# All the engines' orders of a fused attention and gated-MLP kernel written anew

## The chip, the core and the metric

The kernel runs on one core of a Trainium2 chip. The core has a matrix engine (TensorE, "PE" in the profile, with its weight loads as "PEld"), a vector engine (VectorE, "DVE"), a scalar engine (ScalarE, "ACT"), a general engine (GpSimd, "POOL") and a sync engine (SyncE, "SP") that here issues nearly all DMA transfers. Each engine works through its own list of instructions in order and waits on semaphores for the others. SBUF is the working memory, PSUM the eight banks in which TensorE leaves its results. The metric is the device time of one execution in microseconds (us).

## The reference

A linear attention with decay feeds a gated MLP with a spatial mixing matrix. With B = 4 batches, H = 8 heads, S = 768 positions, D = 64 per head, model width 512 and d_ff 1024:

```python
# attention, in blocks of 64 positions
intra = einsum('bhij,bhjd->bhid', einsum('bhic,bhjc->bhij', qb, kb) * Dmask, vb)
inter = einsum('bhid,bhde->bhie', qb * lam_pow, kv_state)
out[:, :, sl] = intra + inter
kv_state = lam_block * kv_state + einsum('bhsd,bhse->bhde', kb * rev_pow, vb)
# gated MLP on x = attention with its heads side by side (4 x 768 x 512)
h = maximum(x @ w_in, 0);  u, v = h[..., :512], h[..., 512:]
v_n = (v - mean(v)) / sqrt(var(v) + 1e-6)
v_s = einsum('ts,bsd->btd', w_spatial, v_n) + b_spatial[None, :, None]
result = (u * v_s) @ w_out
```

All inputs and the result are float32; TensorE multiplies in bfloat16.

## The kernel before, in words

The work is cut into twelve **steps** of 256 positions, three to a batch: step n belongs to batch n // 3. A step loads its keys, queries and values (512 KB each), scales keys and queries by the decay, transposes both, forms scores, masks them, multiplies by the values, adds the carried state, and sends the result through W_in. Each input has three buffers and most intermediates two, used in turn, so that a load waits until the input of three steps before has been read.

Nothing plans at run time. The order stands in the text `ORDER` (lines 16 to 85): each word is one operation, its numbers, and the engine that does it (T = TensorE, D = VectorE, A = ScalarE, P = GpSimd, S = SyncE). The program reads the words from front to back, so an engine's list is the words with its letter, in the order of the text:

```python
        for token in ORDER.split():
            name, *args, e = token.split(".")
            ops[name](e, *map(int, args))
```

The words that matter here (first number the step n, or for the MLP's second half the batch; the last numbers of a T word are PSUM banks):

- **LK, LQ, LV** n (line 196): load keys, queries, values. **WH.0, WH.1** (L253): the two pieces of W_in's v half; **WH.2, WH.3**: the two pieces of its u half. **WQ.0 to 5** (L274): six pieces of W_spatial, 384 KB each; **WP** (L283): W_out. All on SP's queue. The pieces land in float32 in shared buffers and are cast by **CW** (v half), **CX** (u half), **WC** (W_spatial), **WX** (W_out), lines 181 to 185 by the engine. WQ.0 and WQ.1 reuse the buffer of WH.0 and WH.1, WQ.4 and WQ.5 that of WH.2 and WH.3, so that their issue waits for the casts.
- **lam, BR** (ACT's queue): decay rates and the spatial bias. LB, LN, LL, LX make the decay tables; BB, BE spread the bias; **FL** (L309) are matmuls on ones whose result is not used.
- **KM, QM** (L331): keys or queries times decay, on D or P. **TK, TQ** (L366): their transposes on TensorE, **EK, EQ** their copies out of PSUM; from step 7 on **DK, DQ** (L344, L348) transpose by DMA instead, issued by SP. **VC, VD**: cast of the values.
- **SC** (L396) scores, **MK** (L401) mask, **AV** (L459, L468) values, **KP** (L425) state products, **SX, SY, SA** copies and sums of the state. **EX** copies the step's result out as x transposed; **FN** is a copy of one element that orders the two banks.
- **PV, EV** (L493, L498/L500): x times the v half, and its relu. **BN, RA, RD, RB** (L508/509, L513, L518, L523): mean, variance, square root, reciprocal, product of both. **VN** (L532 on D, L529 on A): the normalised v. **PU, EU** (L544, L498/L500): the same for u. **GN** (L536) makes POOL wait for a VN.
- **WT, EW** (L556): transposes of W_spatial and their copies; the last number before the bank is the half of the positions. **GP** copies the bias into a bank, **PW** (L570) adds W_spatial times v to it, **GM** (L576) multiplies by u. A batch has eight PW groups, and each needs all six VN of its batch. **PO, EO** (L581), in halves **PH, EH** (L590): W_out and the copy out; **ST, SH** (L604, L600): the stores.

Of the kernel before, what the change touches and what calls it, by code (L numbers as in the profile page):

```python
# [643 lines left out]
```

## Time and profile before

| what | value |
|---|---|
| median of three runs | 143.64 us (143.48 to 143.75) |
| the profiled execution, device time | 144.71 us |
| its span on the engines | 143.0 us |
| TensorE busy, share of the span | 133.8 us, 94% |
| VectorE, ScalarE, GpSimd busy | 115.3, 82.8, 51.9 us |
| moved by DMA | 33.60 MB |

In the rows of the trace the first two columns are start and duration in us; then come engine, line, operation, what is written and read, the shape, and a count where neighbours are merged. A bracket tells how long the engine had stood idle and what released it. Ends of matmuls are modelled and overlap their successors, so the duration of one matmul is longer than its share of the engine. In a row by stage the columns are the stage, its length, the busy time of PE, PEld, DVE, ACT and POOL with counts, the granted clock of TensorE as a share of full speed, the busy share of the DMA engines and the GB/s that they moved. A list by line gives minimum, median and maximum duration in ns, the first and last start, and the shape.

### The profile page before, as it was taken

What the parts mean: (1) busy time and instruction counts of PE and PEld (TensorE: products, weight loads), DVE (VectorE), ACT (ScalarE), POOL (GpSimd) and SP (SyncE); (2) the same over time, 40 slices, a digit from 0 to 9 for tenths busy, and PEclk for the clock granted to TensorE, in tenths of its full rate; (3) what the DMA queues carried; (4) which work ended last, traced back from release to release, by engine and by line L of the source; (5) the groups of instructions that cost most, each with busy time, mean ns of one, the idle gap of its engine ahead of it and who ended that gap; (6) DMA issues with size and microseconds to landing.
All of it is one profiled execution on the core that took longest, in us unless ns stands there. A gap on an engine that the chain in (4) does not pass through costs nothing.

```text
span 143.0 us, 4741 instructions
## 1 busy us (share of the span) xinstructions
PE 133.8 (94%) x1999; PEld 87.7 (61%) x2014; DVE 115.3 (81%) x236; ACT 82.8 (58%) x158; POOL 51.9 (36%) x61
## 2 busy tenths in 40 slices
...
GB/s 87 347 347 346 386 323 315 294 339 313 337 302 344 259 288 324 285 166 290 293 0 78 49 282 354 180 142 238 276 257 126 177 5 117 406 139 0 78 324 185
DMA packets 54617, 33.60 MB, mean 235 GB/s; under 512 B 11715, under 2 KB 49859, under 8 KB 54596
## 3 DMA queue, kind: packets, MB, share of 16 engines
...
q8 instruction: 15, 0.25, 0.7%
...
HBM read 24.38 MB, written 6.29 MB: 215 GB/s over the span
## 4 chain that ended last, share of the span: by engine, by line
PE 83%; DVE 9%; ACT 3%; issue 2%; DVEq 0%; ACTq 0%
PE ps L570 21%; PE ps L581 14%; PE ps L493 13%; PE ps L544 11%; PE ps L396 5%; PE ps L366 5%; PE ps L309 4%; PE ps L468 4%; PE ps L425 3%; PE ps L459 2%; DVE st L508 2%; DVE qc L331 2%; DVE kc L331 2%; DVE vn L532 1%; DVE win_sb L183 1%
## 5 line engine op out<-in xcount | busy, mean ns | idle before, releaser
L570 PE MATMUL ps<-wt_sb,vn 128*128 128x384 bf16 x192 | 33.7, 326 | 0.5 <-ACT vn L529 0.3
L331 POOL TENSOR_TENSOR kc<-k_in,lv 128x512 bf16<-128x512 f32 x20 | 20.5, 1043 | 30.0 <-PE ps L493 11.5
L401 DVE TENSOR_TENSOR a_sb<-ps,m 128x1024 bf16<-128x1024 f32 x24 | 28.4, 1211 | 0.7 <-PE ps L425 0.6
L570 PEld LDWEIGHTS <-vn 128*128 128x128 bf16 x192 | 18.3, 98 | 12.3 <-ACT vn L529 0.6
L544 PE MATMUL ps<-xT,win_sb 128*128 128x256 bf16 x192 | 23.6, 273 | 0.5 <-DVE win_sb L183 0.5
L331 POOL TENSOR_TENSOR qc<-q_in,lqn 128x512 bf16<-128x512 f32 x18 | 19.3, 1090 | 10.2 <-DMA q_in<-in_q_dram 5.2
L493 PE MATMUL ps<-win_sb,xT 128*128 128x512 bf16 x89 | 22.3, 379 | 0.4
L581 PE MATMUL ps<-wout_sb,gT 128*128 128x512 bf16 x84 | 22.1, 379 | 0.4
L576 DVE TENSOR_TENSOR gT<-ps,uT 128x384 bf16<-128x384 f32 x32 | 16.8, 551 | 7.1 <-PE ps L570 6.7
L544 PEld LDWEIGHTS <-win_sb 128*128 128x128 bf16 x192 | 18.4, 98 | 5.1 <-DVE win_sb L183 0.7
L181 ACT ACTIVATE ps<-bsp 128x384 f32<-128x384 f32 x23 | 11.2, 490 | 10.7 <-DVE gT L576 6.7
L508 DVE BATCH_NORM_STATS2 st<-vh 128x6 f32<-128x512 bf16 x24 | 16.2, 676 | 1.1 <-ACT vh L498 1.1
L181 ACT ACTIVATE o_sb<-ps 128x512 f32<-128x512 f32 (+1 forms) x14 | 8.0, 579 | 15.4 <-PE ps L581 14.6
L493 PEld LDWEIGHTS <-xT 128*128 128x128 bf16 x96 | 8.8, 98 | 9.6 <-ACT xT L181 0.8
L498 ACT ACTIVATE vh<-ps 128x512 bf16<-128x512 f32 x20 | 11.7, 600 | 4.9 <-PE ps L493 3.2
L181 ACT ACTIVATE xT<-ps 128x512 bf16<-128x512 f32 x20 | 11.0, 598 | 5.8 <-PE ps L468 5.7
L581 PEld LDWEIGHTS <-gT 128*128 128x128 bf16 x92 | 8.7, 98 | 8.6
L498 ACT ACTIVATE uT<-ps 128x512 bf16<-128x512 f32 x20 | 11.7, 590 | 2.0 <-PE ps L544 2.0
L468 PE MATMUL ps<-a_sb,vb 64*64 64x128 bf16 x384 | 10.2, 220 | 0.3 <-issue 0.3
L396 PE MATMUL ps<-qT,kT 64*64 64x128 bf16 x384 | 9.7, 226 | 0.0
L309 PE MATMUL ps<-ones 128*128 128x256 bf16 x32 | 7.5, 368 | 1.6 <-DVE ones L305 1.5
L185 POOL CAST vb<-v_in 128x1024 bf16<-128x1024 f32 (+1 forms) x6 | 5.8, 965 | 7.8 <-PE ps L468 7.8
...
## 6 DMA issues: line engine op xcount, KB each, us to landing
...
```

The costliest lines, as they stand in the source:

```text
L181: nc.scalar.activation(out=o, in_=i, func=AF.Copy)
L331: vec(e).tensor_tensor(out=dst[n % NCA][:, u].rearrange("p u m o d -> p o (u m) d"), in0=src[n % NIN].rearrange("p (o u) m d -> p o u m d" ...
L396: nc.tensor.matmul(out=pa[o][row(c), w, j], lhsT=kT[n % NTR][row(o), u, j, c * Q64:(c + 1) * Q64], rhs=qv(n, o, u, c), start=(w == 0 and j ...
L401: nc.vector.tensor_tensor(out=a_sb[n % NA][:, i].rearrange("p o w j x -> p o w (j x)"), in0=ps[:, b0:b1 + 1:b1 - b0].rearrange("p o (w y) ...
L468: nc.tensor.matmul(out=po[c ^ o][row(w), c, i], lhsT=vb[n % NCA][row(c), 4 * o + u, j, :], rhs=a[row(c), i, o, w, j, :], start=(r == 0 and ...
L493: nc.tensor.matmul(out=bank(b), lhsT=x[:, slot(c, g)], rhs=win_sb[:, g, DH:DFF], start=(g == 0), stop=(g == NCH - 1))
L498: nc.scalar.activation(out=o, in_=i, func=AF.Relu)
L508: nc.vector.bn_stats(out=st6[p2][:, t], in_=vh[p2][:, t])
L544: nc.tensor.matmul(out=pu[:, f2].rearrange("p (c x) -> p c x", c=2), lhsT=win_sb[:, g, f * P:(f + 1) * P], rhs=x[:, slot(0, g):slot(1, g) ...
L570: nc.tensor.matmul(out=bank(b)[:, 0:HW], lhsT=vn[bb % 2][:, s, f * P:(f + 1) * P], rhs=wt_sb[:, s, i * HW:(i + 1) * HW], start=False, stop ...
L576: nc.vector.tensor_tensor(out=gT[bb % 2][:, f, cols], in0=bank(b)[:, 0:HW], in1=uT[bb % 2][:, f, cols], op=ALU.mult)
L581: nc.tensor.matmul(out=bank(b), lhsT=gT[bb % 2][:, f, t * P:(t + 1) * P], rhs=wout_sb[:, f, :], start=(f == 0), stop=(f == NCH - 1))
```

## The change

Only the text `ORDER` changes. It has 719 words before and after, 213 of them on TensorE with the same matmuls, 81 on SP with the same transfers, and 54 on POOL. Some operations change their engine: DVE gets 215 instead of 211, ACT 156 instead of 160 (among them: CX.0 from POOL to DVE and CX.1 from DVE to POOL; CW.1 from ACT to POOL, CW.3 from ACT to DVE; KM and QM of step 1 from POOL to DVE, QM.3 from DVE to POOL, KM.3.0 from POOL to DVE; VC.2 and VC.3 from DVE to POOL, VC.4, VC.7 and VC.11 from POOL to ACT; EV.0.1, EU.0.1, EW.2.0 and VN.0.0 from ACT to DVE; WC.4 from ACT to DVE, WC.3 from DVE to ACT). The banks are dealt out anew too.

On SP's queue: queries of step 0 go ahead of its keys, and the first values come sixth instead of fifth. WH.2 and WH.3 stand directly behind the values of step 2, WQ.1, WQ.2, WQ.0 behind them, then the queries of step 3, then WQ.3, WQ.4, WQ.5, and only then keys and values of step 3. Before, the order there was LV.2, LQ.3, WH.3, WQ.0, WQ.1, WQ.2, WH.2, LK.3, LK.4, WQ.3, WQ.4, WQ.5. Further down, the values and queries of step 9 move from in front of DQ.7 to behind DQ.8, the values of step 11 from in front of DK.11 to behind DQ.11. On ACT's queue lam goes ahead of the bias. The 32 filler matmuls are spread otherwise, none behind TK.2.0.

```diff
 ORDER = """
-LK.0.S LQ.0.S LQ.1.S LK.1.S LV.0.S LQ.2.S BR.A lam.A tab.0.A msk.P idn.P posk.P one.D row.D FL.2.256.0.1.T
-FL.2.256.5.1.T FL.2.256.3.1.T FL.2.256.4.1.T FL.2.256.1.1.T FL.1.256.3.1.T FL.2.256.5.1.T LB.1.T LN.1.A eps.D mkc.D
-LL.D LX.A KM.0.0.D QM.0.0.D QM.0.1.D KM.0.1.D FL.1.256.6.1.T BB.1.2.T BB.0.0.T TQ.0.0.3.T FL.2.256.1.1.T TK.0.0.6.T
-tab.1.A BE.1.2.A VC.0.A TQ.0.1.4.T TK.0.1.5.T EQ.0.0.3.D EK.0.0.6.D EQ.0.1.4.D EK.0.1.5.D BE.0.0.D FL.1.256.1.1.T
...
-LV.1.S WH.0.S WH.1.S LV.2.S LQ.3.S WH.3.S VD.1.1.P CW.2.P EQ.1.0.1.D SX.0.D EQ.1.1.5.A SY.0.2.A EK.1.1.3.A
...
-MK.1.0.1.2.D MK.1.1.5.6.D EQ.2.0.0.A VD.1.0.A EK.2.1.4.A KP.1.2.T AV.1.0.0.1.T SY.1.2.D SA.1.0.D FN.1.0.1.D
-EK.2.0.3.A SC.2.1.4.5.T FL.1.256.6.1.T CW.0.A CW.1.A SC.2.0.2.3.T AV.1.1.0.1.T WQ.0.S WQ.1.S WQ.2.S WH.2.S WC.0.P
-WC.1.P WC.2.P MK.2.1.4.5.D MK.2.0.2.3.D SA.1.1.D VC.2.D CW.3.A EX.1.1.1.A EX.1.0.0.A PV.0.1.6.T PV.0.0.4.T
-PV.1.0.5.T KP.2.6.T AV.2.0.2.3.T SA.2.0.D EV.0.1.6.A FN.2.2.3.A EV.0.0.4.A GP.0.0.0.1.A PV.1.1.6.T FL.1.256.0.1.T
-AV.2.1.2.3.T EX.2.0.2.A QM.3.1.D QM.3.0.D TQ.3.2.4.T CX.1.D PU.0.1.0.T PU.1.1.2.T EX.2.1.3.A EV.1.1.6.A BN.0.0.D
-EV.1.0.5.A BN.0.1.D RA.0.A EU.0.1.0.A EU.1.1.2.A PV.2.0.3.T PV.2.1.6.T BN.1.1.D BN.1.0.D EV.2.0.3.A RA.1.A
-EV.2.1.6.A WT.0.0.3.T WT.2.0.5.T EW.2.0.5.A PU.2.1.2.T WT.1.0.0.T BN.2.0.D RD.1.D BN.2.1.D VN.1.1.D RD.0.D RB.0.D
-EW.0.0.3.A RA.2.A VN.0.0.A CX.0.P PU.2.0.6.T EU.2.0.6.A VN.0.1.A EW.1.0.0.D RD.2.D LK.3.S PU.1.0.5.T PU.0.0.3.T
-VN.2.0.D VN.1.0.D VN.2.1.D LK.4.S WQ.3.S EU.1.0.5.D GP.0.2.0.6.D EU.2.1.2.A GP.0.1.0.5.A EU.0.0.3.A GP.0.3.0.2.A
-KM.3.0.P WQ.4.S WQ.5.S LV.3.S LQ.4.S LQ.5.S LV.4.S KM.4.0.P QM.4.0.P QM.4.1.P QM.5.0.P QM.5.1.P VC.4.P PW.0.0.0.1.T
-KM.4.1.D KM.3.1.D WC.3.D GM.0.0.0.1.D PW.0.1.0.5.T PW.0.2.0.6.T TK.3.2.0.T WC.4.A EQ.3.2.4.A EK.3.2.0.A WC.5.D
-GM.0.1.0.5.D GM.0.2.0.6.D WT.2.1.3.T WT.0.1.1.T EW.0.1.1.D WP.S VC.3.D EW.2.1.3.A GP.0.1.1.6.A PW.0.3.0.2.T
-WT.1.1.4.T LK.5.S GM.0.3.0.2.D SC.3.1.0.1.T KP.3.5.T SC.3.0.2.3.T MK.3.1.0.1.D EW.1.1.4.A PW.0.1.1.6.T TK.4.2.0.T
...
-MK.5.0.1.2.D KM.6.0.P KM.6.1.P LK.7.S LQ.7.S LQ.6.S KM.7.1.P QM.7.0.P QM.6.0.P QM.6.1.P EX.4.1.0.A EX.4.0.6.A
-PV.4.1.0.T PV.4.0.4.T AV.5.0.1.5.T BN.3.1.D FN.5.1.5.D KP.6.2.T AV.5.1.1.5.T EV.4.0.4.A PO.0.2.4.T PO.0.0.6.T
-EV.4.1.0.A EX.5.1.5.A EX.5.0.1.A BN.3.0.D PV.5.1.0.T PU.5.1.5.T PV.5.0.1.T KM.7.0.P LV.7.S LV.9.S LQ.8.S LQ.9.S
-LK.8.S LV.8.S EO.0.2.4.D EU.3.0.3.A BN.4.1.D RA.3.A RD.3.D GP.1.2.0.4.D GP.1.1.0.3.A SY.6.2.A EV.5.1.0.D
...
-BN.6.1.D PV.6.0.5.T PO.1.2.2.T VC.9.A KM.9.1.P KM.9.0.P PV.7.1.6.T EV.7.1.6.D PV.7.0.4.T AV.8.0.0.1.T KP.9.3.T
-EV.6.0.5.A GP.2.3.1.6.A EV.7.0.4.A FN.8.0.1.D AV.8.1.0.1.T BN.6.0.D BN.7.0.D EX.8.1.1.A EX.8.0.0.A PU.6.0.5.T
...
-RB.8.D LQ.10.S LK.10.S ST.0.0.S LV.10.S DK.9.S LQ.11.S VN.7.0.D VN.6.1.D VN.8.0.D VN.8.1.D GP.2.3.0.5.A EU.8.0.4.A
...
+lam.A BR.A tab.0.A LQ.0.S LK.0.S LK.1.S LQ.1.S LQ.2.S LV.0.S idn.P posk.P msk.P one.D eps.D row.D FL.1.256.5.1.T
+FL.2.256.1.1.T LB.3.T FL.2.256.6.1.T FL.2.256.2.1.T FL.1.256.0.1.T FL.2.256.4.1.T FL.2.256.6.1.T FL.1.256.6.1.T
+FL.1.256.2.1.T LN.3.A BB.0.4.T BB.1.3.T LL.D LX.A QM.0.1.D KM.0.0.D QM.0.0.P BE.0.4.D mkc.D KM.0.1.P TQ.0.1.1.T
+TK.0.1.4.T KM.1.0.D TQ.0.0.6.T TK.0.0.5.T TK.1.0.0.T BE.1.3.A EQ.0.1.1.A EK.0.1.4.A QM.2.1.P QM.2.0.P KM.1.1.D
...
+FL.1.256.4.1.T MK.1.1.0.1.D KP.1.4.T EK.2.0.5.D EQ.2.1.2.D SA.1.0.D WH.1.S CW.2.P LV.2.S AV.1.0.0.1.T EQ.2.0.6.A
+EK.2.1.3.A CW.0.A FN.1.0.1.D SC.2.0.5.6.T SC.2.1.2.3.T WH.2.S WH.3.S WQ.1.S WQ.2.S WQ.0.S AV.1.1.0.1.T EX.1.1.1.A
+EX.1.0.0.A SY.1.4.D SA.1.1.D CW.3.D PV.0.0.4.T PV.1.1.1.T PV.0.1.0.T MK.2.0.5.6.D MK.2.1.2.3.D EV.0.0.4.A VC.2.P
+CX.1.P WC.1.P WC.2.P WC.0.P AV.2.0.5.4.T KP.2.6.T PV.1.0.6.T BN.0.0.D SA.2.0.D CX.0.D tab.1.A FN.2.5.4.A
+AV.2.1.5.4.T EV.1.0.6.A EV.0.1.0.D BN.1.0.D BN.0.1.D EX.2.1.4.A EX.2.0.5.A EV.1.1.1.A BN.1.1.D PU.1.0.2.T PU.0.0.3.T
+EU.0.0.3.A PU.0.1.5.T PV.2.1.6.T RA.1.A RA.0.A EU.0.1.5.D GP.0.0.0.1.A EV.2.1.6.A RD.1.D RD.0.D EU.1.0.2.D VN.1.1.D
+RB.0.D PV.2.0.0.T PU.2.0.4.T WT.1.0.3.T WT.0.0.5.T PU.1.1.6.T EV.2.0.0.A VN.0.1.A GP.0.2.0.2.A BN.2.1.D EW.1.0.3.D
+BN.2.0.D LQ.3.S QM.3.0.P QM.3.1.P WT.2.0.0.T PU.2.1.3.T EU.2.0.4.A EW.0.0.5.A RA.2.A WQ.3.S WC.3.A GP.0.1.0.4.A
+TQ.3.2.5.T WQ.4.S WQ.5.S EU.1.1.6.A EQ.3.2.5.A GP.0.1.1.6.A EU.2.1.3.A VN.0.0.D EW.2.0.0.D RD.2.D VN.1.0.D VN.2.0.D
+VN.2.1.D LK.3.S PW.0.0.0.1.T WC.5.D WC.4.D GM.0.0.0.1.D LV.3.S LQ.4.S VC.3.P QM.4.0.P LK.4.S KM.4.0.P KM.4.1.P
+GN.2.1.P KM.3.0.D GP.0.3.0.3.A PW.0.2.0.2.T WT.0.1.0.T PW.0.1.0.4.T WT.1.1.5.T WT.2.1.1.T EW.0.1.0.D GM.0.2.0.2.D
+KM.3.1.D GM.0.1.0.4.D PW.0.3.0.3.T TK.3.2.0.T QM.4.1.D GM.0.3.0.3.D EW.1.1.5.A EW.2.1.1.A LV.4.S LK.5.S LQ.5.S WP.S
+PW.0.1.1.6.T KP.3.5.T KM.5.0.P KM.5.1.P WX.1.P GM.0.1.1.6.D GP.0.0.1.4.A EK.3.2.0.A SC.3.0.2.3.T SC.3.1.0.1.T
...
+SC.5.0.3.4.T KM.6.0.P VC.6.P KM.6.1.P LQ.6.S LQ.7.S LK.7.S LV.7.S LK.8.S LV.8.S LQ.8.S ST.0.3.S LK.9.S QM.7.1.P
+KM.7.0.P QM.6.1.P QM.6.0.P KM.7.1.P PO.0.0.0.T EX.4.1.5.A EX.4.0.6.A PV.4.1.2.T PV.4.0.1.T SA.5.0.D MK.5.0.3.4.D
+BN.3.0.D AV.5.0.3.5.T FN.5.3.5.D EV.4.1.2.A EV.4.0.1.A KP.6.6.T AV.5.1.3.5.T PO.0.2.4.T TK.6.2.2.T SY.6.6.A BN.3.1.D
+GP.1.1.0.1.A EX.5.1.5.A RA.3.A EX.5.0.3.A EK.6.2.2.A BN.4.1.D RD.3.D BN.4.0.D PV.5.1.6.T EO.0.2.4.D EV.5.1.6.D
...
+SC.7.0.1.2.T AV.6.1.3.4.T SY.7.0.D EX.6.1.4.A PO.1.4.0.T EO.1.4.0.A EX.6.0.3.A PO.1.5.4.T PO.1.0.0.T DK.8.S DQ.8.S
+ST.0.2.S LK.10.S LQ.10.S LV.9.S LQ.9.S KM.9.1.P ST.0.0.S LQ.11.S LV.10.S SA.7.0.D MK.7.1.5.6.D MK.7.0.1.2.D
+EO.1.5.4.A VC.8.P PV.6.1.6.T EV.6.1.6.A EO.1.0.0.D SA.7.1.D AV.7.0.4.3.T FN.7.4.3.A KP.8.6.T SC.8.1.0.1.T
...
+EV.7.0.4.A PO.1.3.3.T PV.7.1.4.T EO.1.3.3.A SA.8.0.D QM.10.0.D BN.6.0.D EV.7.1.4.A RA.6.A BN.7.1.D RD.6.D VC.9.A
+KM.9.0.P LK.11.S DK.9.S QM.9.0.P KM.10.0.P PO.1.2.0.T PU.7.1.1.T AV.8.0.3.5.T KP.9.6.T FN.8.3.5.D BN.7.0.D
...
+SC.10.1.5.6.T SY.10.3.D DK.11.S DQ.11.S LV.11.S ST.1.0.S ST.0.5.S ST.1.4.S ST.0.1.S ST.1.1.S ST.0.4.S EX.9.1.0.A
...
+PU.9.0.4.T VC.11.A EO.2.3.3.A AV.10.0.5.1.T KP.11.6.T EV.9.1.6.D FN.10.5.1.D SA.11.0.D AV.11.0.2.3.T FN.11.2.3.A
...
+PW.3.1.0.2.T GM.3.1.0.2.D PO.3.3.4.T PH.3.5.0.6.T PW.3.2.0.5.T ST.1.5.S EH.3.5.0.6.D GM.3.0.0.0.D PW.3.3.0.3.T
+ST.1.3.S ST.1.2.S EO.3.3.4.D ST.2.4.S ST.2.0.S ST.2.5.S ST.3.3.S SH.3.5.0.S PO.3.4.2.T EH.3.5.1.1.A SH.3.5.1.A
+GM.3.2.0.5.D GM.3.3.0.3.D PO.3.1.6.T PO.3.2.3.T PO.3.0.1.T EO.3.0.1.A EO.3.4.2.D ST.3.4.S EO.3.1.6.D ST.3.1.S
...
 """
```

More of the change, by code (lines that the diff above doesn't have):

```diff
@@ new lines @@
+TK.0.1.4.T KM.1.0.D TQ.0.0.6.T TK.0.0.5.T TK.1.0.0.T BE.1.3.A EQ.0.1.1.A EK.0.1.4.A QM.2.1.P QM.2.0.P KM.1.1.D
+EK.1.0.0.A EK.0.0.5.A SC.0.1.2.3.T FL.2.256.4.1.T QM.1.0.D TQ.1.0.4.T TK.1.1.1.T EK.1.1.1.A QM.1.1.D EQ.0.0.6.D
+TQ.1.1.0.T SC.0.0.5.6.T FL.2.256.1.1.T FL.1.256.1.1.T FL.1.256.1.1.T FL.2.256.1.1.T FL.2.256.1.1.T MK.0.1.2.3.D
+EQ.1.0.4.D VC.0.A MK.0.0.5.6.D KP.0.1.T SC.1.0.2.3.T AV.0.0.4.5.T FL.2.256.6.1.T LK.2.S SX.0.A FN.0.4.5.A SY.0.1.A
+EQ.1.1.0.D MK.1.0.2.3.D SA.0.1.D KM.2.1.P KM.2.0.P AV.0.1.4.5.T SC.1.1.0.1.T LV.1.S VD.1.0.P WH.0.S CW.1.P
@@ new lines @@
+VC.4.A GP.0.2.1.1.A GM.0.3.1.6.D EQ.4.2.5.D GM.0.0.1.4.D EK.4.2.0.A PW.0.2.1.1.T GM.0.2.1.1.D AV.3.0.6.3.T
+FN.3.6.3.A KP.4.2.T SC.4.1.4.5.T AV.3.1.6.3.T SC.4.0.0.1.T SY.4.2.D EX.3.1.3.A TK.5.2.2.T LV.5.S EX.3.0.6.D
+PV.3.1.3.T MK.4.1.4.5.D QM.5.0.D QM.5.1.D EV.3.1.3.A PU.3.1.6.T PV.3.0.4.T PU.3.0.3.T TQ.5.2.5.T WX.0.A SA.4.0.D
+EK.5.2.2.D LK.6.S EU.3.0.3.A EU.3.1.6.A EQ.5.2.5.A PO.0.1.2.T PO.0.3.3.T SA.4.1.D MK.4.0.0.1.D EO.0.1.2.D
+AV.4.0.6.5.T EV.3.0.4.A EO.0.3.3.D FN.4.6.5.A VC.5.P KP.5.6.T SC.5.1.1.2.T MK.5.1.1.2.D LV.6.S AV.4.1.6.5.T
```

71 lines of the change are left out of this document (28 added, 43 removed).

## The prediction

> **What bounds the kernel now.** I read the page's shares and slices first, then its chain, then a table by stage.
>
> ```profile
> span 143.0 us, 4741 instructions
> PE 133.8 (94%) x1999; PEld 87.7 (61%) x2014; DVE 115.3 (81%) x236; ACT 82.8 (58%) x158; POOL 51.9 (36%) x61
> GB/s 87 347 347 346 386 323 315 294 339 313 337 302 344 259 288 324 285 166 290 293 0 78 49 282 354 180 142 238 276 257 126 177 5 117 406 139 0 78 324 185
> PE 83%; DVE 9%; ACT 3%; issue 2%; DVEq 0%; ACTq 0%
> 26.50:36.36 9.86, 9.24 (x79) 7.00 (x81) 9.27 (x24) 8.39 (x18) 4.77 (x5) 1.00 1.02 325
> 36.36:50.00 13.64, 13.17 (x262) 9.41 (x263) 11.88 (x21) 10.33 (x17) 6.79 (x7) 1.00 1.01 310
> 50.00:126.25 76.25, 75.72 (x1166) 48.50 (x1175) 65.43 (x142) 45.42 (x91) 28.18 (x30) 1.00 0.81 209
> 126.25:139.30 13.05, 12.93 (x75) 7.24 (x74) 8.23 (x15) 3.79 (x9) 0.00 (x0) 1.00 0.29 109
> ```
>
> TensorE is the chain (83%). In the stage rows the first column is the length, the second PE's busy time: PE stands still for 0.62, 0.47, 0.53 and 0.12 us, 1.74 in all, from 26.5 to 139.3. The same matmuls are issued after the change, so from 26.5 on a new order can win at most 1.74, of which only 0.65 lies behind 50 us. What it can lose has no such limit. The rest of a gain must come from the start, where DMA moves some 300 GB/s in each of slices 2 to 17 (of 3.6 us) and VectorE joins the chain.
>
> **The stage that can gain.** Timeline of 20 to 37 us (start, duration, engine, line, and in brackets what ended the idle time before):
>
> ```profile
> 19.39 0.61 POOL L185 CAST win_sb<-wst 128x512 bf16<-128x512 f32 x1 [1.50 <-DMA wst<-in_moe_w_in_dram]
> 20.44 2.76 PE L493 MATMUL ps<-win_sb,xT 128*128 128x512 bf16 x11
> 25.38 0.62 PE L366 MATMUL ps<-ident,qc 128*128 128x128 bf16 x8
> 24.70 1.22 POOL L185 CAST wsp_raw<-wst 128x768 bf16<-128x768 f32 x1 [4.70 <-DMA wst<-in_moe_w_spatial_dram]
> 25.16 1.31 DVE L183 CAST win_sb<-wst 128x1024 bf16<-128x1024 f32 x1
> 26.53 1.92 PE L544 MATMUL ps<-xT,win_sb 128*128 128x256 bf16 x16 [0.53 <-DVE win_sb L183]
> 29.86 1.04 POOL L185 CAST win_sb<-wst 128x1024 bf16<-128x1024 f32 x1 [0.56 <-DMA wst<-in_moe_w_in_dram]
> 32.16 0.81 DVE L523 SCALAR_TENSOR_TENSOR nmr<-mv,rstd 128x2 f32<-128x2 f32 x1
> 31.89 1.07 POOL L331 TENSOR_TENSOR kc<-k_in,lv 128x512 bf16<-128x512 f32 x1 [0.99 <-DMA k_in<-in_k_dram]
> 33.54 1.58 DVE L532 TENSOR_SCALAR vn<-vh,mv,rstd 128x512 bf16<-128x512 bf16 x3
> 36.36 2.11 PE L570 MATMUL ps<-wt_sb,vn 128*128 128x384 bf16 x12 [0.26 <-ACT ps L181]
> ```
>
> **1. The start (queries first, lam before the bias row, moved fillers): 0.** lam first lets the decay tables come sooner, and scores may start up to 2 us earlier. V of step 0 lands one load later (about 12.3) and its cast with it. But the first W_in product (20.44) hangs on the second v piece: SP issues it behind the same eight loads as before, so it lands at about 19.35 again (the cast of 19.39 waited for it). Attention of steps 0 to 2 must only be ready by then. New is that its last cast (CW.3) moves from ACT to DVE, behind SY.1 and SA.1.1. ACT's second table load, moved in between EV.0.0 and FN.2, falls into its wait for AV.2. Bounds -0.5 and +0.4; I take 0, the value of an unchanged landing.
>
> **2. u pieces behind V of step 2: -0.65.** V of step 2, WH.2 and WH.3 then land at about 20.8, 22.3 and 23.8 (512 KB each, 1.5 us at the page's 347 GB/s). Before, the u product waited until 26.53. After, DVE sets the pace, so I add up its queue. Durations, from the lists by line (min/median/max in ns) and the groups by shape:
>
> ```profile
> L401 DVE TENSOR_TENSOR a_sb<-ps,m x24: 1201/1213/1225, 11.2 to 114.9; 128x1024 bf16<-128x1024 f32 x24
> L508 DVE BATCH_NORM_STATS2 st<-vh x24: 660/680/695, 26.4 to 123.6; 128x6 f32<-128x512 bf16 x24
> L509 DVE BATCH_NORM_AGGREGATE mv<-st x24: 181/182/183, 27.1 to 124.3; 128x2 f32<-128x6 f32 x24
> L532 DVE TENSOR_SCALAR vn<-vh,mv,rstd x17: 381/406/931, 31.7 to 125.8; 128x512 bf16<-128x512 bf16 x17
> L523 DVE SCALAR_TENSOR_TENSOR nmr<-mv,rstd x8: 139/151/809, 32.2 to 125.4; 128x2 f32<-128x2 f32 x8
> L331 DVE TENSOR_TENSOR kc<-k_in,lv x4: 676/686/1550, 6.1 to 36.7; 128x512 bf16<-128x512 f32 x4
> L500 DVE TENSOR_SCALAR vh<-ps 128x512 bf16<-128x512 f32 x4 | 2.7, 681 | 0.0
> ```
>
> Neighbouring DVE operations overlap by 0.08, so a step is the duration less 0.08. The three maxima, and the 1.31 of 25.16, fall on moments in which POOL was working on SBUF: nmr of 32.16 ended when POOL's kc of 31.89 ended. So a DVE operation on SBUF alone can wait for a POOL operation. CW.3 is triggered with POOL's CW.2 (19.39, 0.61) and goes second: done 20.3. Two masks 2.25 (22.55), BN.0.0 0.80, SA.2.0 0.35 (23.7). CX.0 now stands on DVE and meets POOL's CX.1, released by WH.3 at 23.8: 1.04 of waiting and 0.5 of its own, 25.3. So u products start at 25.3 instead of 26.53, but without TQ.3 (0.5 without its drain, row of 25.38), which is moved behind them: 0.7 ahead. Then EV.0.1 0.60, three BN 2.40, two EU 1.20, two RD 0.2 (29.7); VN.1.1 and RB.0 0.45 with 1.35 of waiting for QM.3 on POOL, whose queries land at about 29 (31.5); two BN 1.6, two EW 0.95, RD 0.1, four VN 1.35 (35.5). The last vn is therefore at 35.5, about as before (33.54 + 1.58 = 35.12), although PE is ready for PW.0 at about 33.7 (25.3, six PU and two PV at 0.86, three WT and TQ.3 1.5). PW.0's first group ends at 35.7 and the next starts at once (its GP is early) where it started at 36.36: -0.65. Ends: without any of these waits vn is ready at 32.9, PE itself sets the start and gains 2.0; with one more POOL operation (VC.3, 1.04) in front of the last VN it loses 0.4. I take the sum, nearest to the rows of 25.16 and 32.16.
>
> The Trainium skill (SBUF — State Buffer, Who interferes with whom) has the port pair that DVE and GpSimd share as an exclusive lock, held for a whole instruction: who issues first has it, the other "fully blocks". By that rule term 2 is -0.65; by a shared bandwidth it would come near -2.0. The trace agrees with the lock (nmr 0.81 instead of 0.15 beside kc).
>
> **3. W_spatial in a row, K and V of step 3 behind it: +0.15.** All six pieces land by about 32 to 33, so the transposes of the second half (WT.*.1) no longer wait for data. But WC.4 and WC.5 stand on DVE right behind the last vn, and POOL starts VC.3 as V of step 3 lands, near 35.8: the same kind of wait, 0 to 0.9, before WT.0.1. On SP, WQ.4 waits for CX.0, and eight loads stand behind it; three transfers in flight cover that: 0. Of the 0.47 that PE loses from 36 to 50 all can go; two waits like it come: SC.3 behind EK.3, which follows GP.0.0.1 on ACT (0.25), SC.4.1 behind GM.0.0.1 on DVE (0.2). Ends 0 and +0.9.
>
> **4. Step 5's second copy (EX.5.0): +0.35.** Lines of before for step 5 and the lengths of what moves in:
>
> ```profile
> 59.34 0.41 PE L468 MATMUL ps<-a_sb,vb 64*64 64x128 bf16 x16
> 59.78 1.09 ACT L181 ACTIVATE xT<-ps 128x512 bf16<-128x512 f32 x2
> 61.42 1.03 PE L493 MATMUL ps<-win_sb,xT 128*128 128x512 bf16 x4
> L181 ACT ACTIVATE ps<-bsp 128x384 f32<-128x384 f32 x23 | 11.2, 490 | 10.7 <-DVE gT L576 6.7
> L513 ACT ACTIVATE rstd<-mv,eps_t x12: 286/296/306, 28.1 to 124.6; 128x2 f32<-128x2 f32 x12
> ```
>
> Before, both copies followed AV.5.1 at once and were ready at 60.87; two PO groups hid them (1.67 to 61.42, so 0.86 a group). After, GP.1.1.0 (0.49) stands before the first and RA.3 (0.2 a step) before the second, so they end 1.8 behind AV.5.1, and PE's cover is PO.0.2 and TK.6, 1.35 (0.86 and 0.5). Ends 0 (GP done before AV.5.1 ends) and 0.5.
>
> **5. V of step 9 behind the transpose of step 8: +0.5.** Before, SP issued it with V of step 7, by 57.4. After, it is the fourth transfer behind DQ.8, and SP stands at DQ.8 until AV.6.1 has read qT.
>
> ```profile
> 53.96 3.45 SPq L196 DMA_DIRECT2D v_in<-in_v_dram  x2
> 78.95 1.23 SPq L348 DMA_TRANSPOSE qT<-qc  x1
> 83.21 0.42 PE L396 MATMUL ps<-qT,kT 64*64 64x128 bf16 x16
> DMA to landing us min/median/max: 2.7/4.2/4.9
> 85.45 1.06 ACT L181 ACTIVATE vb<-v_in 128x1024 bf16<-128x1024 f32 x1
> 85.54 2.04 POOL L331 TENSOR_TENSOR kc<-k_in,lv 128x512 bf16<-128x512 f32 x2 [11.51 <-PE ps L493]
> ```
>
> DQ.8 was issued at 78.95 and SC.8, which needs it, ran at 83.21; the transposes took 4.2 to land (median, middle row). The POOL product that needs the first load behind it started 2.3 later (85.54), which bounds that landing from above. So, counted from SC.8's start, K of step 10 lands at 2.2 and 0.8 for the store ahead of it, Q of 10 1.5 later, V of 9 at 6.0, and VC.9 (1.06) ends at 7.1. PE reaches KP.9 at 6.6: SC, AV, SC, AV about 1.4, six groups of 0.86 5.2. Wait 0.5, and EO.1.2, EX.8.0 and the rest of ACT stand behind VC.9. DQ.8 itself has about the cover that it had, 4. Ends 0 (it lands as fast as the least row, 2.7) and 0.9. V of step 11 goes behind DQ.11 in the same way, with 7.3 of cover for 6: nothing.
>
> **6. The remainder: +0.1.** The 0.65 still open behind 50 us can be won in part, and small waits (AV.6.0 behind GM.1.0.0, PV.4.1 behind EX.4) come in; ends -0.3 and +0.6. At the end one PO (0.86) instead of two hides GM.3.3.0 (shorter than a mask): enough, 0. The other moves between ACT, DVE and POOL change busy times of engines that have idle time in every stage row: 0.
>
> **Sum:** -0.65 + 0.15 + 0.35 + 0.5 + 0.1 = +0.45. The profiled execution took 144.71, 1.07 over the median of the runs; it would become 145.2, the median 143.64 becomes 144.1.
>
> **Rivals.**
> *Faster:* DVE is not held up. If CX.0 gets in ahead of CX.1 and queries of step 3 land behind VN.1.1, the last vn is ready near 33.7 and term 2 is -1.9; with terms 3 to 6 at +0.15, +0.25, +0.4 and +0.1 the time is 142.6. It decides at the last vn: before 35.0 (gain 1.1) the change wins. For it: POOL works only 4.77 of the 9.86 us there, so most DVE operations meet nothing. Against: POOL's work moves into just this stretch.
> *No change:* about half of that, 143.6; gain and new waits cancel. W_spatial "in a row" would then do nothing, as the vn came last already.
> *Clock:* half a clock window more at the start. These rows (granted clock in the third column from the right) show it:
>
> ```profile
> 5.17:8.58 3.41, 2.69 (x19) 1.53 (x18) 2.68 (x5) 2.29 (x5) 0.70 (x1) 1.00 1.15 346
> 8.58:12.00 3.42, 2.47 (x41) 1.71 (x42) 3.42 (x7) 1.06 (x1) 3.42 (x4) 0.50 1.15 347
> 18.80:22.20 3.40, 3.35 (x115) 2.15 (x102) 3.35 (x7) 3.40 (x8) 0.61 (x1) 1.00 1.00 303
> ```
>
> After 0.72 of idle in one 3.41 window the next ran at 0.50. After the change no filler is left between AV.1.1 and the first PV, where PE may idle about 1 us; one half window costs up to 1.7 of matmul time (half of 3.41), less some 0.3 that waits anyway, on top of the sum: 145.5. The Trainium skill (TensorE: Matmul & The Clock Gate, Part 1) says that the clock falls after an idle window of about 3.4 us; by that this rival would be nothing, but the rows above do not agree.
>
> **How the numbers follow.** Forecast (slower by a little) 0.39, faster rival 0.34, no change 0.17, clock 0.10. 0.2% is 0.29 us, about what this measurement can tell from no change. So faster 0.34, same 0.17, slower 0.49. The likeliest case alone is 143.9 to 144.8; the range reaches from the faster rival, 142.5, to the clock case, 145.4.
>
> **What would show it.** The u product's first start (25.3), the last vn (35.5) and DVE operations longer than their medians beside POOL; PE's wait at PV.5.1 on xT, and at KP.9 on vb with VC.9 started by a DMA. If PE starts PW.0 before 34 and none of the waits in 4 and 5 is there, the forecast is wrong.

## The result, and the profile after

The changed kernel takes 153.66 us (median of four executions, 151.51 to 154.66), the kernel before 143.69 beside it: a ratio of 1.054, with a 95% interval of 1.047 to 1.062. The forecast of 144.1 had the sign right, and was about 9.5 us too low. The profiled execution, the longest of the four, took 154.66 us, against 144.71 of the one before. These lines of its page answer to the first ones shown of before (span, busy time, granted clock in 40 slices, the chain by engine):

```profile
span 152.9 us, 4742 instructions
PE 137.2 (90%) x1999; PEld 88.8 (58%) x2014; DVE 125.1 (82%) x240; ACT 80.0 (52%) x154; POOL 54.4 (36%) x61
PEclk9999999999999999999569999999999999999999
PE 27%; DVE 7%; DMA 2%; issue 2%; ACT 1%; SPq 1%; POOL 1%
```

VectorE is busy for 10 us more with only four operations more, and in two slices near the middle TensorE's clock was at about half. The chain of this page is followed back only to 87.6 us, so its 27% for TensorE can't be set beside the 83% of before. Next, three of the stages, cut at the same events in both kernels (start of the second PW.0 group, 50 us, first PW.1, end of PW.1, end of PW.2). The columns are length, busy time of PE, PEld, DVE, ACT and POOL, granted clock, DMA share and GB/s. After:

```profile
35.85:50.00 14.15, 13.73 (x271) 9.82 (x270) 13.01 (x21) 9.60 (x17) 10.04 (x9) 1.00 1.04 321
...
68.32:84.76 16.44, 12.31 (x90) 6.31 (x92) 12.82 (x14) 5.39 (x10) 4.84 (x5) 0.79 0.20 30
84.76:116.12 31.36, 28.86 (x457) 17.86 (x464) 28.19 (x54) 16.14 (x32) 12.26 (x12) 1.00 0.78 188
```

The last two of them before:

```profile
69.26:77.90 8.64, 8.64 (x87) 5.07 (x88) 6.39 (x11) 2.36 (x4) 4.77 (x6) 1.00 0.50 100
77.90:106.50 28.60, 28.39 (x461) 18.10 (x467) 24.86 (x53) 17.65 (x35) 11.24 (x12) 1.00 1.04 220
```

The second group of PW.0 starts at 35.85 instead of 36.36, and PW.1 at 68.32 instead of 69.26. Of this 0.94, 0.86 is the group PO.0.4, which the new order does later, inside PW.1. So up to here the new order is level. Then PW.1 takes 16.44 instead of 8.64, which is 7.80 more, and the stretch to the end of PW.2 takes 31.36 instead of 28.60, 2.76 more. The rest differs by 0.06 up to PW.3 and by 0.22 behind it. The sum is -0.51 - 0.43 + 7.80 + 2.76 + 0.06 + 0.22 = 9.90, the difference of the spans.

**PW.1.** Timeline of after, by engine, around 68 us:

```profile
67.72 5.60 DVE L532 TENSOR_SCALAR vn<-vh,mv,rstd 128x512 bf16<-128x512 bf16 x2
67.87 0.30 POOL L536 CAST seen<-vn 1x1 f32<-1x1 bf16 x1 [5.01 <-DVE vn L532]
68.13 2.03 POOL L331 TENSOR_TENSOR kc<-k_in,lv 128x512 bf16<-128x512 f32 x2
70.13 3.03 POOL L331 TENSOR_TENSOR qc<-q_in,lqn 128x512 bf16<-128x512 f32 x3
68.32 0.98 PE L570 MATMUL ps<-wt_sb,vn 128*128 128x384 bf16 x5
73.37 6.92 PE L570 MATMUL ps<-wt_sb,vn 128*128 128x384 bf16 x25 [4.08 <-DVE vn L532]
```

GN.5.0 (the second row) held POOL until VN.5.0, the last vn but two of batch 1. At 68.17 it let go, and POOL ran five products on SBUF without a pause, KM.8.1, KM.8.0, QM.8.0, QM.7.0 and QM.8.1, until 73.16. VN.5.1, the last vn, had been issued at 68.04 and ended at 73.31, 5.27 us later. PW.1.2.0 did five of its six matmuls and then waited 4.08 for it. Before, KM.8.0 and KM.8.1 still waited for TK.6 at this point and started at 68.89, behind the last vn. These are the rows of before:

```profile
68.34 0.40 DVE L532 TENSOR_SCALAR vn<-vh,mv,rstd 128x512 bf16<-128x512 bf16 x1
68.89 2.04 POOL L331 TENSOR_TENSOR kc<-k_in,lv 128x512 bf16<-128x512 f32 x2 [3.87 <-PE ps L366]
```

The third column from the right of these windows of after is the granted clock:

```profile
65.22:68.63 3.41, 3.41 (x32) 2.63 (x31) 2.71 (x8) 2.26 (x5) 0.76 (x2) 1.00 0.22 46
68.63:72.04 3.41, 0.66 (x5) 0.20 (x2) 3.41 (x1) 2.03 (x5) 3.41 (x4) 1.00 0.00 0
72.04:75.45 3.41, 2.08 (x7) 1.04 (x8) 2.66 (x4) 0.49 (x1) 1.12 (x2) 0.50 0.34 77
75.45:78.87 3.42, 3.42 (x13) 1.60 (x11) 2.17 (x4) 1.96 (x3) 0.00 (x0) 0.50 0.00 0
```

In the window from 68.63 TensorE worked for 0.66 of 3.41, and the next two windows ran at 0.50. So the 7.80 is 4.08 of waiting, 2.85 of slower matmuls (12.31 busy against 9.46 in the run below that keeps its clock) and the 0.86 of PO.0.4.

**Step 9 and PW.2.** After, ACT's and TensorE's rows at KP.9, and VectorE's at the vn of batch 2:

```profile
97.01 1.04 ACT L181 ACTIVATE vb<-v_in 128x1024 bf16<-128x1024 f32 x1
98.10 0.45 PE L425 MATMUL ps<-vb,kc 64*64 64x64 bf16 x32 [1.05 <-ACT vb L181]
100.54 1.21 DVE L532 TENSOR_SCALAR vn<-vh,mv,rstd 128x512 bf16<-128x512 bf16 x1
105.51 2.53 DVE L532 TENSOR_SCALAR vn<-vh,mv,rstd 128x512 bf16<-128x512 bf16 x3
```

KP.9 waited 1.05 for VC.9. The queries of step 9 landed behind its values, and POOL's QM.9.0 started only at 99.56. POOL's products of steps 9 to 11 came beside the vn of batch 2: three vn took 2.53 (1.05 in a run below where none is held up), and TensorE waited 0.62 and 0.55 in PW.2.1.0. Together these waits are 2.22 of the 2.76.

### The profile page after: what moved, and what is told of

It is laid out like the page before. It is cut to its first block, busy times and chain, and to the rows that moved or that the text cites. A ratio compares the mean times of both kernels' runs of the same rounds, so it can differ in the third digit from the quotient of the medians.

```text
span 152.9 us, 4742 instructions
## 1 busy us (share of the span) xinstructions
PE 137.2 (90%) x1999; PEld 88.8 (58%) x2014; DVE 125.1 (82%) x240; ACT 80.0 (52%) x154; POOL 54.4 (36%) x61
## 5 line engine op out<-in xcount | busy, mean ns | idle before, releaser
L570 PE MATMUL ps<-wt_sb,vn 128*128 128x384 bf16 x192 | 36.9, 344 | 5.3 <-DVE vn L532 5.3
L570 PEld LDWEIGHTS <-vn 128*128 128x128 bf16 x192 | 19.0, 103 | 19.2 <-DVE vn L532 6.4
L331 POOL TENSOR_TENSOR kc<-k_in,lv 128x512 bf16<-128x512 f32 x19 | 21.7, 1149 | 15.1 <-issue 12.4
L331 POOL TENSOR_TENSOR qc<-q_in,lqn 128x512 bf16<-128x512 f32 x16 | 17.4, 1102 | 17.1 <-issue 11.0
L581 PE MATMUL ps<-wout_sb,gT 128*128 128x512 bf16 x83 | 21.0, 379 | 1.5 <-issue 1.3
L532 DVE TENSOR_SCALAR vn<-vh,mv,rstd 128x512 bf16<-128x512 bf16 x19 | 14.3, 788 | 0.0
L185 POOL CAST vb<-v_in 128x1024 bf16<-128x1024 f32 (+1 forms) x7 | 7.5, 1068 | 12.1 <-DMA v_in<-in_v_dram 7.3
L498 ACT ACTIVATE uT<-ps 128x512 bf16<-128x512 f32 x17 | 9.9, 593 | 2.7 <-PE ps L544 2.7
```

What stands on the lines that cost most here:

```text
L331: vec(e).tensor_tensor(out=dst[n % NCA][:, u].rearrange("p u m o d -> p o (u m) d"), in0=src[n % NIN].rearrange("p (o u) m d -> p o u m d" ...
L498: nc.scalar.activation(out=o, in_=i, func=AF.Relu)
L532: vec(e).tensor_scalar(out=vn[p2][:, t], in0=vh[p2][:, t], scalar1=mv[p2][:, t, 0:1], scalar2=rstd[p2][:, t:t + 1], op0=ALU.subtract, op1= ...
L570: nc.tensor.matmul(out=bank(b)[:, 0:HW], lhsT=vn[bb % 2][:, s, f * P:(f + 1) * P], rhs=wt_sb[:, s, i * HW:(i + 1) * HW], start=False, stop ...
L581: nc.tensor.matmul(out=bank(b), lhsT=gT[bb % 2][:, f, t * P:(t + 1) * P], rhs=wout_sb[:, f, :], start=(f == 0), stop=(f == NCH - 1))
```

## Experiments

Theory A: an operation of VectorE on SBUF that meets a row of POOL's operations there waits for the whole row, and this, with the clock that falls in the wait, and the late loads of step 9, made the loss. Rival B: the new order of the loads or the new start costs the time. Rival C: a vn waits for one POOL operation, and the rest of the 5.27 has another cause. The experiments ran in three groups on three chips, and the kernel before, run beside each group, took 145.24, 144.54 and 144.77, so ratios to it are compared. In some of these kernels the text of the order has one or two lines fewer, and line numbers are smaller by as much.

**The changed kernel again.**

> The changed kernel once more, unaltered, beside the other runs of this call. Theory A: ratio 1.05 to 1.07 to the kernel before, VN.5.1 again about 5.3 us with five products in POOL's row. If VN.5.1 were 0.4 here, the loss of the first execution was chance.

Ratio 1.063 (1.055 to 1.072), all four executions between 152.7 and 154.95. VN.5.1 took 5.27 again, PE waited 4.08, and PW.1 took 16.33. The first execution was no chance.

**POOL held until the last vn.**

```diff
-GN.5.0.P KM.8.1.P KM.8.0.P QM.8.0.P
+GN.5.1.P KM.8.1.P KM.8.0.P QM.8.0.P
```

> The changed kernel with one word altered: GN.5.0 becomes GN.5.1, so POOL's five products (KM.8.1, KM.8.0, QM.8.0, QM.7.0, QM.8.1) start behind VN.5.1, the last vn of batch 1, and not behind VN.5.0. Theory A (VN.5.1 lost its port to the whole row of POOL, and the matrix clock fell in the wait): VN.5.1 takes about 0.41 us, PW.1 runs without its 5.3 of waiting and at full clock, so 153.66 becomes about 146.8 (146.0 to 147.8); the losses at KP.9 and at the vn of batch 2 stay. Rival B (the loads in their new order or the start cost the time): no change, 151.5 to 154.7. Rival C (a vn waits for one POOL operation and the rest of its 5.27 has another cause): about 152.5.

147.48 us, ratio 1.016 (1.010 to 1.022). PW.1 as one window:

```profile
69.85:79.36 9.51, 9.46 (x90) 5.47 (x92) 7.96 (x14) 5.13 (x10) 5.17 (x6) 1.00 0.31 57
```

The last two vn of batch 1 in its timeline, merged into one row:

```profile
69.25 0.73 DVE L531 TENSOR_SCALAR vn<-vh,mv,rstd 128x512 bf16<-128x512 bf16 x2
```

One changed number takes PW.1 from 16.44 to 9.51 and wins back the larger part of the loss. Rivals B and C are out as its cause: the loads and the start are those of the changed kernel.

**One and three products ahead of the hold.** GN.5.0 stays, and GN.5.1 is added behind the first, or behind the third, product of the row.

```diff
-GN.5.0.P KM.8.1.P KM.8.0.P QM.8.0.P
+GN.5.0.P KM.8.1.P GN.5.1.P KM.8.0.P QM.8.0.P
```

> The changed kernel with one word added: behind GN.5.0 POOL does one product (KM.8.1), then waits in GN.5.1 for VN.5.1, then the other four. Theory A in its strong form (a vn on VectorE waits until POOL has nothing more to run at once): VN.5.1 lasts one product and its own 0.4, about 1.4 us instead of 5.27, PE waits about 1 us and keeps its clock; the time stands about 1 us over the run with the hold ahead of the row (147.5), so 148.5 (147.6 to 149.5). If the 5.27 has nothing to do with the number of products in the row, VN.5.1 stays at 4 to 5 us and the time above 151.

> The changed kernel with GN.5.1 added behind the third product of POOL's row (KM.8.1, KM.8.0, QM.8.0, then the hold, then QM.7.0, QM.8.1). One product gave VN.5.1 1.27, five gave 5.27. Theory A (the vn waits until POOL stops): 3 products, 3.3 (3.1 to 3.5), PE waits about 2.9 at PW.1. The clock had fallen behind waits of 2.0 and 4.1 and had not behind 1.0 and 1.8; so it falls here, and the time is about 3 and 1.5 over the run with one product: 1.045 of before (1.035 to 1.055). Without a fall of the clock 1.037.

With one product 147.81, ratio 1.023 (1.017 to 1.029); its last two vn:

```profile
68.81 1.59 DVE L532 TENSOR_SCALAR vn<-vh,mv,rstd 128x512 bf16<-128x512 bf16 x2
69.22 1.03 POOL L331 TENSOR_TENSOR kc<-k_in,lv 128x512 bf16<-128x512 f32 x1
```

With three, 147.79, ratio 1.021 (1.014 to 1.027); the same place:

```profile
68.95 3.60 DVE L532 TENSOR_SCALAR vn<-vh,mv,rstd 128x512 bf16<-128x512 bf16 x2
71.36 1.03 POOL L331 TENSOR_TENSOR qc<-q_in,lqn 128x512 bf16<-128x512 f32 x1
72.68 0.18 POOL L536 CAST seen<-vn 1x1 f32<-1x1 bf16 x1 [0.29 <-DVE vn L532]
```

PW.1 of that run as a window:

```profile
69.55:81.31 11.76, 9.63 (x90) 5.38 (x92) 10.73 (x14) 5.28 (x10) 5.02 (x6) 1.00 0.28 43
```

The pair of vn takes 0.73 with no product beside it, 1.59 with one, 3.60 with three and 5.60 with five: about 1.0 us for each product. That is theory A's step, as these four traces show it. Two things came out otherwise. PE waited 2.08 with three, and the clock did not fall (1.00 in the window). And the execution of which this trace is took 150.10, while the other three took 147.1 to 147.9, no longer than with one product. There is no trace of them here, so the value for three stands on one execution. VN.5.1 is issued only 0.1 ahead of POOL's first product, so it may have come through there; that isn't shown.

**The fault put into the kernel before.** Nothing of the new loads or the new start is in it.

```diff
-QM.6.1.P ... KM.7.0.P ... QM.7.1.P KM.8.0.P KM.8.1.P VC.7.P QM.8.1.P GN.2.1.P QM.8.0.P
+QM.6.1.P ... GN.4.0.P KM.7.0.P QM.7.1.P KM.8.0.P KM.8.1.P VC.7.P QM.8.1.P QM.8.0.P
```

> The kernel before with the suspected fault put in, and neither the new loads nor the new start: on POOL, GN.2.1 becomes GN.4.0 and stands, followed by KM.7.0, ahead of QM.7.1 (KM.7.0 came two words before). So POOL's row KM.7.0, QM.7.1, KM.8.0, KM.8.1, VC.7, QM.8.1, QM.8.0 starts at about 67.7, just before VN.3.0, the last vn of batch 1. Theory A: VN.3.0 waits for the whole row or most of it (4 to 7 us instead of 0.41), PW.1 waits for it, and the clock falls: 148 to 153. Rival C (one operation at a time): at most 1 us more, 144.7. Rival B: no change but for the later products, 143.5 to 144.3.

152.07, ratio 1.044 (1.037 to 1.052). VN.3.0, and the first row and the last (of two operations) of the seven POOL operations beside it:

```profile
67.73 6.65 DVE L531 TENSOR_SCALAR vn<-vh,mv,rstd 128x512 bf16<-128x512 bf16 x1
...
67.21 1.03 POOL L330 TENSOR_TENSOR kc<-k_in,lv 128x512 bf16<-128x512 f32 x1
...
72.19 2.03 POOL L330 TENSOR_TENSOR qc<-q_in,lqn 128x512 bf16<-128x512 f32 x2
```

Two clock windows of the same run:

```profile
68.62:72.04 3.42, 0.19 (x4) 0.02 (x1) 3.42 (x1) 1.40 (x2) 3.42 (x4) 1.00 0.39 87
72.04:75.45 3.41, 1.01 (x4) 0.51 (x5) 2.67 (x2) 0.00 (x0) 2.19 (x3) 0.50 0.31 70
```

In the old order the row, with the fall of the clock, cost 6.8 us over the kernel before on that chip: a ratio of 1.044, against 1.054 and 1.063 for the whole change. TensorE waited 5.62 for VN.3.0, which ended at 74.38, when the row ended (74.22).

**Fillers in the wait.** The row is left in, and TensorE is kept at work until VN.5.1 is done.

```diff
-TQ.6.2.0.T PW.1.2.0.5.T PW.1.1.0.1.T EU.4.0.3.A EU.5.0.2.A
+TQ.6.2.0.T EU.4.0.3.A FL.44.256.3.1.T PW.1.2.0.5.T PW.1.1.0.1.T EU.5.0.2.A
```

> The changed kernel with POOL's row left as it is, and 44 filler matmuls of 256 columns (some 4.7 us) on TensorE between TQ.6 and PW.1.2.0, in bank 3 behind EU.4.0.3. They change no operand of anything; only TensorE is kept at work while VN.5.1 waits. If the fallen clock costs by itself: VN.5.1 still takes about 5, the granted clock stays at 1.0, the groups PW.1.1.0, PW.1.2.1 and PW.1.0.1 take 1.0 each instead of 2.0, and the time falls by about 2.2 from that of the changed kernel, to a ratio of about 1.04 to before. If the lower clock hides behind the other engines: no change, 1.054.

The text above was off in one thing: the fillers use the bank in which PW.1.2.1 finds its bias, and this kernel most likely leaves a part of that bias out. No instruction of the changed kernel is missing. 154.49, ratio 1.061 (1.053 to 1.068). The wait and what followed:

```profile
68.90:73.40 4.50, 4.26 (x41) 3.75 (x39) 4.50 (x1) 2.25 (x5) 4.50 (x5) 1.00 0.00 0
73.40:83.52 10.12, 10.12 (x96) 6.01 (x97) 8.24 (x14) 2.94 (x5) 0.26 (x1) 1.00 0.24 53
```

The clock stayed at 1.00, and from the end of the wait PW.1 ran as fast as with the hold. So here the fall comes from the idle time. The whole time did not follow: in the traced execution (156.03) TensorE waited 1.32 and 0.55 for the vn of batch 2, and the clock fell to 0.5 there instead (from 107.51, for 3.41). But two other executions, whose mean clock was 0.996 and 1.000, took 153.04 and 153.24, within the 151.51 to 154.95 of the changed kernel. The price of the fall at PW.1, 2.85, therefore rests on the busy time in the windows. That it lengthens the whole time is not shown; some of it may hide behind other waits.

**Values and queries of step 9 early, alone and with the hold.**

```diff
-LK.9.S QM.7.1.P KM.7.0.P QM.6.1.P QM.6.0.P KM.7.1.P ... DQ.8.S ST.0.2.S LK.10.S LQ.10.S LV.9.S LQ.9.S
+LK.9.S QM.7.1.P KM.7.0.P QM.6.1.P QM.6.0.P KM.7.1.P LV.9.S LQ.9.S ... DQ.8.S ST.0.2.S LK.10.S LQ.10.S
```

> The changed kernel with LV.9 and LQ.9 moved on SP's queue from behind ST.0.2 (after DQ.8) to behind LK.9 (ahead of DK.7); nothing else. Theory A: KP.9 no longer waits for VC.9 (about 1.05) and POOL's row of step 9 to 11 runs ahead of the vn of batch 2, which no longer wait (about 1.5), so 153.66 becomes about 151.0 (150.3 to 152.0); the wait at VN.5.1 stays. Rival B: no change. By the prediction's own term for this move only 0.5 comes back: 153.2.

> Both edits: the hold until VN.5.1, and V and Q of step 9 ahead of DK.7. Theory A: both losses go, 144.2 (143.5 to 145.2), that is within 1 us of the kernel before; what is left over is step 5's second copy and the start. Rival B: 151 to 154. If the two edits do not add up, there is a third cause.

Alone 155.11, ratio 1.067 (1.060 to 1.074); with the hold 149.31, ratio 1.033 (1.023 to 1.043), worse than the hold alone. This part of theory A's expectation was wrong. The run with the loads alone, its vn as one group by line (minimum, median and maximum in ns):

```profile
L530 DVE TENSOR_SCALAR vn<-vh,mv,rstd x19: 382/404/5271, 30.1 to 136.0; 128x512 bf16<-128x512 bf16 x19
```

The longest is VN.5.1 again. Two windows at its PW.2:

```profile
104.14:107.55 3.41, 1.34 (x10) 0.61 (x8) 3.41 (x5) 1.79 (x4) 2.61 (x3) 1.00 0.54 122
107.55:110.96 3.41, 3.41 (x13) 1.56 (x12) 3.01 (x7) 0.49 (x1) 0.00 (x0) 0.50 0.00 0
```

KP.9 waited only 0.35. But POOL's row from VC.10 to QM.11.1 met the vn of batch 2 all the same, TensorE stood still for 2.07 in PW.2.1.0, and one window at half clock followed. In the run with both edits the wait was 1.76; its PW.2 as a window:

```profile
98.81:109.57 10.76, 8.97 (x86) 4.89 (x87) 10.56 (x18) 2.69 (x6) 2.21 (x3) 1.00 0.26 58
```

Three vn of batch 2 in its timeline:

```profile
98.91 2.58 DVE L530 TENSOR_SCALAR vn<-vh,mv,rstd 128x512 bf16<-128x512 bf16 x3
```

So the late loads were not the cause of the second collision. They only set where in the row it falls.

**Both edits and a hold for batch 2.** The five operations move behind VN.8.1, and GN.8.1 goes ahead of them.

```diff
+VN.8.1.D GN.8.1.P VC.10.P KM.10.1.P KM.11.1.P QM.10.1.P KM.11.0.P
```

> The run with both edits (hold until VN.5.1, V and Q of step 9 early) and, in addition, POOL's row VC.10, KM.10.1, KM.11.1, QM.10.1, KM.11.0 behind a GN.8.1 that waits for the last vn of batch 2. Theory A: the run with both edits was no better than the hold alone only because the earlier loads brought that row beside the vn of batch 2 (PE waited 1.76 at PW.2); with the hold this wait goes and the vn there take 0.41: about 146.7 (146.0 to 147.6), 0.8 below the hold alone. If the early loads cost by themselves (transfers in each other's way), it stays at 148.5 to 149.5.

146.19, ratio 1.016 (1.009 to 1.023). PW.2 in the same cut as above:

```profile
98.19:106.93 8.74, 8.74 (x86) 5.06 (x87) 8.54 (x17) 2.69 (x6) 7.16 (x8) 1.00 0.40 90
```

10.76 became 8.74, and the ratio fell from 1.033 to 1.016, so the early loads by themselves are not what made the run with both edits worse. It is no better than the hold alone, where the vn of batch 2 fell into a pause of POOL's row. KP.9 still waited 0.85, now not for the load but for ACT, where VC.9 stands behind RA.6.

**Three small edits on top.** VC.9 goes behind EX.7.1, GN.2.1 ahead of VC.3, and PW.0.2.1 with its GM behind KP.4.

```diff
-VC.3.P QM.4.0.P LK.4.S KM.4.0.P KM.4.1.P GN.2.1.P
+GN.2.1.P VC.3.P QM.4.0.P LK.4.S KM.4.0.P KM.4.1.P
-PW.0.2.1.1.T GM.0.2.1.1.D AV.3.0.6.3.T FN.3.6.3.A KP.4.2.T SC.4.1.4.5.T
+AV.3.0.6.3.T FN.3.6.3.A KP.4.2.T PW.0.2.1.1.T GM.0.2.1.1.D SC.4.1.4.5.T
```

> The former kernel and three small edits: VC.9 on ACT directly behind EX.7.1 (it stood behind RA.6, and KP.9 waited 0.47 for it), GN.2.1 on POOL ahead of VC.3 (so that no vn of batch 0 meets it; VN.2.0 took 1.15 in three runs), and PW.0.2.1 with its GM.0.2.1 behind KP.4 on TensorE (a wide group among small matmuls, where TensorE stood without any engine to wait for, 0.28 to 1.87 us in AV.3.1). Expected 145.3 (144.5 to 146.3): level with the kernel before, whose runs on that chip were 145.2. If it ends below 144.7 the new order is worth something once POOL stays away from the vn; if above 146.5, some loss is still unfound.

147.51, ratio 1.017 (1.011 to 1.024), a miss: the hold put POOL's row beside another operation of VectorE, KM.3.0.

```profile
36.44 4.19 DVE L331 TENSOR_TENSOR kc<-k_in,lv 128x512 bf16<-128x512 f32 x1
...
36.04 1.03 POOL L185 CAST vb<-v_in 128x1024 bf16<-128x1024 f32 x1
37.05 1.03 POOL L331 TENSOR_TENSOR qc<-q_in,lqn 128x512 bf16<-128x512 f32 x1
38.05 2.03 POOL L331 TENSOR_TENSOR kc<-k_in,lv 128x512 bf16<-128x512 f32 x2
```

KM.3.0 took 4.19 (1.06 in after) and TK.3 came late. So it is not only the vn: a product with two inputs in SBUF is held up in the same way.

**The same without the hold ahead of VC.3, and with VC.3 on ACT.**

```diff
-VC.3.P QM.4.0.P LK.4.S KM.4.0.P KM.4.1.P GN.2.1.P KM.3.0.D GP.0.3.0.3.A
+QM.4.0.P LK.4.S KM.4.0.P KM.4.1.P GN.2.1.P KM.3.0.D GP.0.3.0.3.A VC.3.A
```

> The kernel with both edits and the hold for batch 2, plus VC.9 directly behind EX.7.1 on ACT, plus PW.0.2.1 with GM.0.2.1 behind KP.4; GN.2.1 stays where the changed kernel has it. In the run that also moved GN.2.1 ahead of VC.3, POOL's row VC.3, QM.4.0, KM.4.0, KM.4.1 came beside KM.3.0 on VectorE, which took 4.19 instead of 0.7 (TK.3 waited 1.0 for it). Without that edit: KP.9 no longer waits 0.85, AV.3.1 no longer 0.36, and no new wait: about 1.2 below 146.2 on that chip, a ratio to before of 1.007 (1.002 to 1.013). If it stays at 1.016, the small edits are worth nothing.

> The former kernel with VC.3 moved from POOL to ACT, directly behind GP.0.3.0. VN.2.1 (1.20 in the run with the hold for batch 2, where VC.3 started at the landing of its values) then takes 0.41, and PW.0 starts up to 0.4 earlier: ratio 0.003 below that of the former kernel, 1.004 (0.998 to 1.010). If QM.4.0, now alone on POOL, holds up WC.5 or KM.3.0 instead, no gain or a loss up to 1 us.

146.26, ratio 1.010 (1.006 to 1.014), and 145.88, ratio 1.010 (1.005 to 1.015); VC.3's engine makes no difference. In the first of them no vn is held up any more; all of its vn as a group:

```profile
L532 DVE TENSOR_SCALAR vn<-vh,mv,rstd x19: 382/407/411, 30.8 to 126.4; 128x512 bf16<-128x512 bf16 x19
```

With the collisions of the vn undone, the new order is still 1% behind the old one: no version here beats the kernel before. Other operations of VectorE are still longer beside one operation of POOL in that trace: CW.3 took 1.04 (0.42 in after), and CX.0 1.27 (0.72 in the run with the loads alone).

## Why the prediction was wrong, step by step

- **The sign.** It was right by chance: most of the loss lies at a term that the sum had at 0.
- **Start (0).** The first W_in product came at 19.94, 0.50 earlier than before and at the end of the bounds. A stop of TensorE until 24.37 that waited for no engine (1.44, below) took that away again.
- **u pieces early (-0.65).** Right in size, by luck: the last vn of batch 0 ended at 35.38 (forecast 35.5), and the second PW.0 group started 0.51 earlier. On the way two errors cancelled. CX.0 ended 1.05 later than worked out, at 26.35, so the first u product came at 26.45 and not at 25.3; what held it up was less POOL than SA.2.0 ahead of it on VectorE, which waited for KP.2 until 25.12, behind the same stop of TensorE. And QM.3 did not hold up VN.1.1 and RB.0, which the sum had charged with 1.35 (they took 0.40 and 0.15). The mechanism, a wait for POOL, was the one that made the loss elsewhere, but its price, one POOL operation per wait, was too low there: POOL can take its whole row.
- **W_spatial in a row (+0.15).** Stopped time in the stage fell from 0.47 to 0.42; no wait at SC.3 or SC.4.1 is seen, only 0.28 in AV.3.1. Within its ends. The prediction's own parts do not add up to +0.15, though: -0.47, 0.25 and 0.2 make -0.02, and the wait of 0 to 0.9 behind VC.3 is left without a value.
- **Step 5's second copy (+0.35).** Wrong. PV.5.1 did not wait for it. TensorE lost 0.8 one group earlier, at PO.0.2, for no engine (below). The lengths that the prediction gives, 1.8 less 1.35, make 0.45 and not 0.35.
- **V of step 9 (+0.5).** KP.9 waited 1.05 in the first trace (the end given was 0.9) and 0.40 in the second of the same kernel: the size was about right. What it left out is that the queries land behind the values, and what POOL then does late.
- **The remainder (+0.1).** This is the step that failed. It said that moves among ACT, DVE and POOL on engines with idle time cost 0. The new order puts GN.5.0 ahead of KM.8.1 and so let POOL's row loose at VN.5.0, at the moment in which the last vn of batch 1 ran; the row before had been kept away by its wait for TK.6. Term 2 had been walked through vn by vn; the same walk was not made for batches 1 and 2. PW.1 alone measured +6.9, the stretch to the end of PW.2 +2.8.
- **Rivals.** The clock rival had the right mechanism at the wrong place: between AV.1.1 and the first PV the clock stayed at 1.00, but two windows at half came behind PW.1's wait, 2.85 instead of up to 1.7. (The trace of after has no record of the clock ahead of 14.0, so the 9s of the page's first slices say nothing; four 128x128 matmuls, 0.39 at full clock (before, at 7.91), took 0.61 at 8.11 and 0.63 at 12.18, so TensorE ran slowly there, and the first W_in product came early all the same.) The faster rival and no change are out.

The Trainium skill (SBUF — State Buffer, SBUF: two separate sides) says of the port pair that who starts first has it "for the whole instruction". The trace agrees that it is exclusive, but here VN.5.1 waited through five instructions of the other engine. What decides between one and all is open: at the vn of batch 2 in the trace of after, VN.7.1 and VN.8.1 took 1.16 and 1.13 instead of 0.41, less than one product more each, beside a row that went on.

Open is also the last 1%: in the trace of the last kernel but one 0.7 us is a stop at PO.0.2 (below), and TensorE waits 0.5 and 0.3 for the casts of W_in on VectorE; the rest was not traced to single waits.
